# Attention followed by a rational feed-forward network on one core: VectorE runs both heads' passes over the scores in a row, ahead of the copies that read the transposes

## The chip, the core and the metric

The kernel runs on one core of a Trainium2 chip. A core has five engines with queues of their own that are worked off in order: TensorE (PE in the rows, PEld for its weight loads), VectorE (DVE), ScalarE (ACT), GpSimd (POOL) and SyncE (SP, which here only issues DMAs). They meet at semaphores alone. The metric is the device time of one execution in microseconds; less is better.

## The reference, cut to what matters

```
scores = (q @ k^T) / 8 + bias(head, i, j)      # B=4, H=8, S=576, D=64, f32
attn   = softmax(scores)                       # over j
x      = (attn @ v), heads side by side        # 2304 x 512
h      = x @ w_in                              # 2304 x 2048
g      = P(h) / Q(h)                           # cubic over quadratic
out    = g @ w_out                             # 2304 x 512
```

The bias is a small network of the distance of i and j. It is the same for all batches, so the kernel first writes it to DRAM as tables.

## The kernel before, in words

The first stage (lines 561 to 659) makes the bias tables. The second is attention, the third the feed-forward network. The change touches attention alone.

Attention works on units. A unit is a pair of heads of one batch: 16 units. A unit has 576 query rows; rows come in blocks of 128, and two units share one block for their last 64 rows. So there are 72 steps, nine for every two units (the list `steps`; NS is 72). In step i the function `step_a` writes out work of four different blocks, so that each engine has something of another block to do:

- TensorE: the scores of block i (`e_qk`, line 324): head 0 of the pair uses rows 0 to 63 of the array, head 1 rows 64 to 127. The scores come in two halves of 288 columns, in the order head 0, head 1, head 0, head 1. Each f32 product is two records in the trace, so a step has 8. Then the transposes of the probabilities of block i-2 (`e_tp`, line 393; 18 of them), then the product with v of block i-3 (`e_pv`, line 433; 20 records).
- VectorE: one pass over each head's scores (`e_ttr`, line 334): it adds the bias, writes -scores to `s2` and takes the row minimum into `m`. Between the pass of head 0 and that of head 1 stand the "tails" of block i-2 (line 412, and line 416 where a unit ends): copies of the last transposes out of the accumulator tile `mx`. Behind both stand the reciprocals of the row sums where a unit ends (`e_recip`, lines 360 and 361), the copy of block i-3's product with v out of `mx` (line 443), and at last one of three passes that split weights into a high and a low part (lines 130, 138, 144; the "weight pass", given out one to a step by `run_jobs`).
- ScalarE: the exponential of head 1 of block i-1 (line 350), a rebias of the weights in every third step (line 135), the copy of block i-2's other transposes out of the tile `tp` (line 401), and the exponential of head 0 of block i.
- GpSimd multiplies a finished unit by the reciprocals (`e_norm`) and subtracts for the low weights. SyncE issues the loads of q, k, v, bias and weights and the stores, in the order in which the program writes them.

What sets the order around the change are the buffers. The scores have one tile for each head (`ps_sc`, two buffers), so head j's scores of step i+1 can't start before head j's pass of step i is through. `mx` has one buffer: the transposes of step i+1 write it when the copies at lines 412 and 443 of step i have read it. The tails wait for TensorE's last write of `mx` that was written out ahead of them, which is the last record of the product with v at line 433, although they read other columns. The tile `s2` has three buffers, so head 1's pass of step i reuses what the exponential of head 0 of step i-1 has read.

Of the kernel before, what the change touches and what calls it, by code (L numbers as in the profile page):

```python
# [33 lines left out]
def tile_attn_moe(  # L34
# [183 lines left out]
    with tc.manual_schedule():  # L218
# [3 lines left out]
        with ExitStack() as actx:  # L222
# [54 lines left out]
            def split_x(n_, k, x=None):  # L277
                if k == 0:
                    pool = xps[n_ % 2]
                    xh[n_] = pool.tile([P, KD, TT], F32R, tag="xh", name=f"xh{n_}")  # L280
                    xl[n_] = pool.tile([P, KD, TT], F32R, tag="xl", name=f"xl{n_}")
                hi, lo = (v[n_][:, k, :] for v in (xh, xl))
                x = xr[n_][:, k, :] if x is None else x
                return (
                    lambda: A.copy(out=hi, in_=x),
                    lambda: V.tensor_tensor(out=lo, in0=x, in1=hi.bitcast(F32), op=ALU.subtract),  # L286
                )
# [23 lines left out]
            def e_qk(i):  # L311
                u, c = steps[i]
                for j in range(2):
                    sc[i, j] = ps_sc.tile([P, 2, 512], F32, tag="sc", name=f"sc{i}_{j}")
                if c < 4:
                    ops = [(u, slice(c * P, c * P + P), slice(0, P))]
                else:
                    ops = [(u + z, slice(512, S), slice(64 * z, 64 * z + 64)) for z in range(2)]
                for a in range(2):
                    for j in range(2):  # L320
                        r = slice(64 * j, 64 * j + 64)
                        for n, x, o in ops:
                            q, k = qk[n]
                            T.matmul(  # L324
                                sc[i, j][o, a, :SH], q[r, x], k[r, a * SH:(a + 1) * SH],
                                start=True, stop=True,
                            )

            def e_ttr(i, j):
                u, c = steps[i]  # L330
                p, b = units[u]
                t = epool.tile([P, S], F32, tag="s2", name=f"s2_{i}_{j}", bufs=3)
                m = epool.tile([P, 1], F32, tag="m", name=f"m{i}_{j}", bufs=4)
                V.tensor_tensor_reduce(  # L334
                    out=t.rearrange("p (a s) -> p a s", a=2),
                    in0=sc.pop((i, j))[:, :, :SH],
                    in1=bias[p][:, 5 * j + c, :].rearrange("p (a s) -> p a s", a=2),
                    scale=-0.125, scalar=3.0e38,
                    op0=ALU.add, op1=ALU.min, accum_out=m,
                )  # L340
                s2[i, j] = (t, m)

            def e_exp(i, j):
                u, c = steps[i]
                if j == 0:
                    prob[i] = epool.tile([P, 2 * S], F32, tag="p", name=f"p{i}")
                t, m = s2.pop((i, j))
                k = 4 * j + c if c < 4 else 8 + j
                z = 1 - j
                A.activation(  # L350
                    out=prob[i][:, z * S:z * S + S], in_=t, func=AF.Exp,
                    bias=m, scale=-1.0, accum_out=sums[u % 4][:, k:k + 1],
                )
# [4 lines left out]
            def e_recip(u):  # L358
                sm = sums[u % 4][:, 0:nsum(u)]
                V.tensor_scalar(out=sm, in0=sm, scalar1=1e-9, scalar2=None, op0=ALU.add)  # L360
                V.reciprocal(out=sm, in_=sm)

            def load_rb(u):
                t = rb[u] = npool.tile([P, S], F32, tag="rb", name=f"rb{u}", bufs=1)
                z = 64 * (u % 2)
                for j in range(2):
                    o = t[64 * j:64 * j + 64]
                    r, rl = rsum[u], rsum[u - u % 2]
                    nc.sync.dma_start(
                        out=o[:, 0:512].rearrange("d (c s) -> d c s", c=4),  # L370
                        in_=r[4 * j:4 * j + 4, :].unsqueeze(0).to_broadcast([64, 4, P]),
                    )
                    nc.sync.dma_start(
                        out=o[:, 512:S],
                        in_=rl[8 + j:9 + j, z:z + 64].to_broadcast([64, 64]),
                    )

            def e_norm(u):
                x = xs.pop(u)
                p, b = units[u]  # L380
                eng = V if u == NX else G
                eng.tensor_tensor(out=x, in0=x, in1=rb.pop(u), op=ALU.mult)
                nc.sync.dma_start(out=xd[b][:, p, :], in_=x)
# [71 lines left out]
            def run_act():  # L455
                while actq:
                    actq.pop(0)()
# [10 lines left out]
            def loads(i):  # L468
                g, c = divmod(i, UPG)
                if i == 1:  # L470
                    load_qk(1, nc.scalar)
                    load_v(1, nc.scalar)
                for u, x, y in ((2 * g + 2, 0 if g else 4, 3 if g else 6), (2 * g + 3, 5 if g else 7, 8)):
                    if u < NU and c == x:
                        load_qk(u)
                    if u < NU and c == y and u != 3:
                        load_v(u)
                if i == UPG + 1:
                    load_v(3)
                p, r = divmod(i, 2 * UPG)  # L480
                r = {2: 0, 7: 1, 11: 2, 13: 3, 16: 4}.get(r)
                if r is not None and p + 1 < NP:
                    load_bias(p + 1, r)
                if i == NS - 14:
                    load_x(0, 0, 0, KD - 1)
                if i == NS - 6:
                    load_x(1, 1, 0, KD - 1)

            def step_a(i):
                def ok(d):  # L490
                    return 0 <= i - d < NS

                if i < NS:
                    loads(i)
                first = []
                if NS - i in (11, 9, 7):
                    first = split_x(0, (11 - NS + i) // 2)
                elif i == NS - 5:
                    first = split_x(0, KD - 1, x12[0][:, :TT])
                if first:  # L500
                    first[0]()
                    later.append(first[1])
                while len(later) > (1 if first else 0):
                    later.pop(0)()
                if ok(0):
                    e_qk(i)
                if ok(1):
                    e_exp(i - 1, 1)
                run_act()
                if i >= TL:  # L510
                    mx = ps_mx.tile([P, 2, 512], F32, tag="mx", name=f"mx{i}")
                tails = pv = None
                if ok(TL):
                    tails = e_tp(i - TL, mx)
                if i == NS + 1:
                    mm1(0, 1)
                if ok(TL + 1):
                    pv = e_pv(i - TL - 1, mx)
                if ok(0):
                    e_ttr(i, 0)  # L520
                if tails:
                    tails()
                if ok(0):
                    e_ttr(i, 1)
                    e_exp(i, 0)
                if ok(1):
                    u, c = steps[i - 1]
                    if c == (3 if u % 2 else 4):
                        e_recip(u)
                if i == NS - 1:  # L530
                    mm1(0, 0)
                if i == NS + 1:
                    load_x(1, 1, KD - 1, KD)
                g, c = divmod(i - TL, UPG)
                if g > 0:
                    u = 2 * g - 2
                    if c == 0 and u != NX:
                        e_norm(u)
                    if c == 5 and g * 2 < NU:
                        e_norm(u + 1)  # L540
                    if c == 1 and u + 1 < NU - 1:
                        load_rb(u + 1)
                if i == NS - 7:
                    x12.append(xs[NX])
                    e_norm(NX)
                if g < NU // 2 and c == (6 if g else 8):
                    load_rb(2 * g)
                if i == NS + TL:
                    load_rb(NU - 1)
                if pv:  # L550
                    pv()
                if i >= 2:
                    run_jobs(i >= 5 and (c > 0 or g % 2 == 0))
# [383 lines left out]
```

## Time and profile before

| | us |
|---|---|
| median of 3 runs | 766.61 (766.08 to 766.80) |
| the profiled execution | 766.36 |
| its span | 764.6 |
| steps 6 to 69 of attention (63 steps) | 71.53 to 338.39 |
| attention's end and the feed-forward network | 338.39 to 764.60 |

The profiled execution took 1.8 us more than its span, for what lies around it. A step is counted here from the start of head 0's pass over the scores to that of the next step: 266.86 us for 63 steps, 4.24 us each. All times in the rows are microseconds from the start of the span.

### The profile page before, as it was taken

Reading aid. Unit: us, or ns where it says so; the run is one execution under the profiler, and the core shown is the slowest. Engines: PE = TensorE matmul, PEld = TensorE weight load, DVE = VectorE, ACT = ScalarE, POOL = GpSimd, SP = SyncE. Lnnn points to the kernel's source line nnn. Section 1 sums busy time; section 2 is a strip of 40 time slices with the busy share of each in tenths; the row PEclk is TensorE's granted clock in tenths of the full one; section 3 lists DMA queues with packets and bytes.
Section 4 is the critical chain, followed back from the end, with each engine's and each line's share of the span. In section 5 each row is a group of like instructions: output and inputs, shape, how many; then the busy total and the mean of one; then the engine's idle time right before and its main releaser. Section 6 shows DMA issues by size and latency. Waiting matters only on the chain.

```text
span 764.6 us, 16662 instructions
## 1 busy us (share of the span) xinstructions
PE 715.1 (94%) x6450; PEld 599.4 (78%) x6450; DVE 574.5 (75%) x1032; ACT 495.0 (65%) x758; POOL 232.8 (30%) x144
## 2 busy tenths in 40 slices
PE   7998888888888888888999999999999999999997
PEld 4766666666666666667989989989998998999896
DVE  7985555655565556663999999999997878787766
ACT  6887666666767666766765767576675656556552
POOL 0010121211212121111634554545544444543442
PEclk9999999999999999999999999999999999999999
DMA  5787687675858777561445433337972122130121
GB/s 178 282 310 273 197 274 234 201 224 180 276 156 274 210 233 243 170 192 47 148 140 174 168 125 125 132 143 235 311 251 85 41 83 80 46 123 35 50 83 42
DMA packets 77583, 129.50 MB, mean 169 GB/s; under 512 B 12208, under 2 KB 33856, under 8 KB 77504
## 3 DMA queue, kind: packets, MB, share of 16 engines
q1 hardware_dynamic: 76640, 126.77, 50.9%
q10 hardware_dynamic: 864, 1.67, 0.7%
q8 instruction: 51, 0.84, 0.4%
q14 instruction: 28, 0.23, 0.1%
HBM read 89.65 MB, written 35.61 MB: 164 GB/s over the span
## 4 chain that ended last, share of the span: by engine, by line
PE 55%; DVE 5%; issue 1%; ACT 0%; POOL 0%; DVEq 0%; POOLq 0%
PE o L767 24%; PE h L300 24%; PE mx L433 3%; PE sc L324 2%; PE tp L393 1%; DVE s L334 1%; DVE gh L715 1%; DVE m L722 0%; PE mx L393 0%; DVE t L705 0%; DVE xl L286 0%; DVE pt L412 0%; DVE wk L144 0%; DVE t L708 0%; POOL gl L736 0%
## 5 line engine op out<-in xcount | busy, mean ns | idle before, releaser
L324 PE MATMUL sc<-k,q 64*128 64x288 f32 (+1 forms) x640 | 138.5, 434 | 37.1 <-DVE m L334 25.6
L697 POOL TENSOR_TENSOR u<-u,w 128x768 f32<-128x768 f32 x48 | 96.6, 2013 | 162.3 <-ACT u L695 162.3
L324 PEld LDWEIGHTS sc<-k,q 64*128 64x128 f32 (+1 forms) x640 | 69.6, 174 | 83.7 <-issue 75.3
L350 ACT ACTIVATE p<-s,m 128x576 f32<-128x576 f32 x144 | 111.8, 776 | 33.0 <-DVE m L334 32.7
L334 DVE CUSTOM_DVE_ANT_0 s<-sc,bias 128x576 f32<-128x576 f32 x144 | 107.9, 750 | 23.2 <-PE sc L324 16.1
L401 ACT COPY pt<-tp 128x1024 f32<-128x1024 f32 x72 | 72.9, 1012 | 66.5 <-PE tp L393 66.4
L694 ACT ACTIVATE w<-h 128x768 f32<-128x768 f32 x48 | 39.0, 813 | 101.6 <-PE h L300 101.6
L736 POOL TENSOR_TENSOR gl<-m,r 128x768 fp32r<-128x768 f32 x47 | 87.2, 1856 | 57.5 <-DVE m L729 55.4
L412 DVE COPY pt<-mx 128x128 f32<-128x128 f32 x72 | 21.0, 291 | 106.7 <-PE mx L433 106.7
L300 PE MATMUL h<-xl,wih 128*128 128x384 f32 x288 | 97.0, 337 | 0.3 <-DVE xl L286 0.3
L300 PE MATMUL h<-xh,wih 128*128 128x384 f32 x288 | 97.3, 338 | 0.0
L300 PE MATMUL h<-xh,wil 128*128 128x384 f32 x288 | 97.0, 337 | 0.0
L433 PE MATMUL mx<-pt,v 128*64 128x128 f32 (+1 forms) x1600 | 95.1, 267 | 0.9 <-DVE xs L443 0.9
L767 PE MATMUL o<-woh,gh 128*128 128x512 f32 x216 | 85.3, 395 | 0.0
L767 PE MATMUL o<-wol,gh 128*128 128x512 f32 x216 | 85.1, 394 | 0.0
L433 PEld LDWEIGHTS mx<-pt,v 128*64 128x64 f32 x1600 | 78.6, 137 | 6.0 <-ACT u L695 1.1
L393 PE MATMUL tp<-ident,p 64*128 64x64 f32 x1152 | 74.7, 228 | 0.0
L701 ACT ACTIVATE r<-u,qc 128x768 f32<-128x768 f32 x48 | 45.1, 940 | 36.7 <-POOL u L697 36.4
L705 DVE TENSOR_TENSOR t<-t,h 128x768 f32<-128x768 f32 x48 | 45.5, 949 | 30.4 <-ACT t L696 24.9
L393 PEld LDWEIGHTS tp<-ident,p 64*128 64x128 f32 x1152 | 61.8, 139 | 6.2
L722 DVE SCALAR_TENSOR_TENSOR m<-u,qc,gh 128x768 f32<-128x768 f32 x48 | 61.7, 1285 | 5.0
L729 DVE SCALAR_TENSOR_TENSOR m<-t,cst,m 128x768 f32<-128x768 f32 x48 | 64.2, 1337 | 1.7
(73 smaller groups left out, 1354.6 us busy)
## 6 DMA issues: line engine op xcount, KB each, us to landing
tab<-e SPq DMA_DIRECT2D x36, 295.5 KB, 4.2
wx<-in_w_in_dram SPq DMA_DIRECT2D x16, 512.0 KB, 5.1
wy<-in_w_in_dram SPq DMA_DIRECT2D x16, 512.0 KB, 4.3
wx<-in_w_out_dram SPq DMA_DIRECT2D x16, 512.0 KB, 3.9
wy<-in_w_out_dram SPq DMA_DIRECT2D x16, 512.0 KB, 5.2
xr<-xd SPq DMA_DIRECT2D x7, 768.0 KB, 6.2
ws<-wh SPq DMA_DIRECT2D x20, 256.0 KB, 2.2
ws<-wl SPq DMA_DIRECT2D x20, 256.0 KB, 2.9
```

The lines of the kernel that those rows point to most:

```text
L300: T.matmul(hps[s][:, j, :TT], w[:, k, sl], x[:, k, :], start=(k == 0 and z == 0), stop=(k == KD - 1 and z == 2),)
L324: T.matmul(sc[i, j][o, a, :SH], q[r, x], k[r, a * SH:(a + 1) * SH], start=True, stop=True,)
L334: V.tensor_tensor_reduce(out=t.rearrange("p (a s) -> p a s", a=2), in0=sc.pop((i, j))[:, :, :SH], in1=bias[p][:, 5 * j + c, :].rearrange(" ...
L350: A.activation(out=prob[i][:, z * S:z * S + S], in_=t, func=AF.Exp, bias=m, scale=-1.0, accum_out=sums[u % 4][:, k:k + 1],)
L393: T.transpose(out, pb[x, k0:k0 + P], ident[x, x])
L401: A.copy(out=t[:, 0:8].rearrange("p x (r s) -> p r x s", r=2), in_=ps)
L433: T.matmul(ps[y, o], vt[n][:, kc, y], t[:, 2 * kc + j if kc < 4 else 8, o], start=(kc == 0), stop=(kc == 4),)
L697: G.tensor_tensor(out=u, in0=u, in1=w, op=ALU.mult)
L722: V.scalar_tensor_tensor(out=m, in0=rt[s, "u"], scalar=qc, in1=rt[s, "gh"].bitcast(F32), op0=ALU.add, op1=ALU.mult,)
L729: V.scalar_tensor_tensor(out=m, in0=rt[s, "t"], scalar=abs_[:, 0:1], in1=m, op0=ALU.add, op1=ALU.subtract)
L736: eng.tensor_tensor(out=lo, in0=rt[s, "m"], in1=rt[s, "r0"], op=ALU.mult)
L767: T.matmul(po[n, c], l[:, j, c * P:(c + 1) * P], r[fp][:, j, :], start=(first and x is a), stop=(last and x is z),)
```

## The change

In each step, head 1's pass over the scores (`e_ttr(i, 1)`) now stands directly behind head 0's, and the tails stand behind the reciprocals and GpSimd's norms and the loads that go with them, directly ahead of the copy of the product with v. No instruction is added or taken out.

```
                 if ok(0):
-                    e_ttr(i, 0)
-                if tails:
-                    tails()
-                if ok(0):
-                    e_ttr(i, 1)
+                    for j in range(2):
+                        e_ttr(i, j)
                     e_exp(i, 0)
                 if ok(1):
                     u, c = steps[i - 1]
...
                 if g < NU // 2 and c == (6 if g else 8):
                     load_rb(2 * g)
+                if tails:
+                    tails()
                 if i == NS + TL:
                     load_rb(NU - 1)
                 if pv:
```

VectorE's queue in step 41, before. `s2_41_0` is written by the pass of head 0 (its second row reads out the minimum), `s2_41_1` by that of head 1, `pt39` by the tails, `xs8` by the copy of the product with v, `wh5` by the weight pass:

```order
L334 ISA s2_41_0_3333,m41_0_3334<-sc41_0_3292,bias2_2016 128x576
L334 ISA m41_0_3334 128x1
L412 COPY pt39_3302<-mx41_3301 128x128
L334 ISA s2_41_1_3337,m41_1_3338<-sc41_1_3293,bias2_2016 128x576
L334 ISA m41_1_3338 128x1
L360 TENSOR_SCALAR sum0_113<-sum0_113 128x10
L361 RECIPROCAL sum0_113<-sum0_113 128x10
L443 COPY xs8_3209<-mx41_3301 128x128
L138 SCALAR_TENSOR_TENSOR wh5_1_3299<-wx5_1_3048,wh5_1_3299 128x512
```

The same step on VectorE, after:

```order
L334 ISA s2_41_0_3333,m41_0_3334<-sc41_0_3292,bias2_2016 128x576
L334 ISA m41_0_3334 128x1
L334 ISA s2_41_1_3336,m41_1_3337<-sc41_1_3293,bias2_2016 128x576
L334 ISA m41_1_3337 128x1
L360 TENSOR_SCALAR sum0_113<-sum0_113 128x10
L361 RECIPROCAL sum0_113<-sum0_113 128x10
L412 COPY pt39_3302<-mx41_3301 128x128
L443 COPY xs8_3209<-mx41_3301 128x128
L138 SCALAR_TENSOR_TENSOR wh5_1_3299<-wx5_1_3048,wh5_1_3299 128x512
```

The copy out of `mx` moved from between the two passes to behind the reciprocals; the rest kept its order.

TensorE's queue in step 42, before, with the semaphores that a row waits for. `sc42_0` and `sc42_1` are the scores of the two heads, `p40` the probabilities that are transposed, `pt39` what the product with v reads:

```order
L324 MATMUL sc42_0_3346<-k9_2740,q9_2739 128x288 [waits DVE_49]
L324 MATMUL sc42_1_3347<-k9_2740,q9_2739 128x288 [waits DVE_49,PE_49]
L324 MATMUL sc42_0_3346<-k9_2740,q9_2739 128x288
L324 MATMUL sc42_1_3347<-k9_2740,q9_2739 128x288
L393 MATMUL mx42_3353<-ident_60,p40_3282 128x64 [waits DVE_49,PE_49,Activation_49]
```

And after:

```order
L324 MATMUL sc42_0_3346<-k9_2740,q9_2739 128x288 [waits DVE_49]
L324 MATMUL sc42_1_3347<-k9_2740,q9_2739 128x288 [waits DVE_49]
L324 MATMUL sc42_0_3346<-k9_2740,q9_2739 128x288
L324 MATMUL sc42_1_3347<-k9_2740,q9_2739 128x288
L393 MATMUL mx42_3353<-ident_60,p40_3281 128x64 [waits DVE_49,PE_49,Activation_49]
```

TensorE's order is the same; head 1's first product no longer waits for TensorE's own earlier work (the last product with v, which the tails had waited for).

On SyncE the store of a finished unit's row sums, which belongs to the tails, moves behind loads in two places: near the start, and at the end of attention. The second, before:

```order
L419 DMA rs15_5248<-rt15_5247 8x128
L274 DMA xr1_4819<-xd0_72 128x192
L274 DMA xr1_4819<-xd1_73 128x192
L383 DMA xd2_74<-xs14_4862 128x576
L369 DMA rb15_5292<-rs15_5248 64x512
```

And after:

```order
L274 DMA xr1_4819<-xd0_72 128x192
L274 DMA xr1_4819<-xd1_73 128x192
L419 DMA rs15_5248<-rt15_5247 8x128
L383 DMA xd2_74<-xs14_4862 128x576
L369 DMA rb15_5292<-rs15_5248 64x512
```

The last unit's sums are stored behind two loads of the feed-forward network's input instead of ahead of them.

## Rows read from the trace of the kernel before

**Rows 1.** The page's first part: busy time, share of the span, instructions.

```profile
PE 715.1 (94%) x6450; PEld 599.4 (78%) x6450; DVE 574.5 (75%) x1032; ACT 495.0 (65%) x758; POOL 232.8 (30%) x144
```

**Rows 2.** Stretches: length, busy PE, PEld, DVE, ACT, POOL, granted clock, DMA share, GB/s.

```profile
71.53:338.39 266.86, 233.83 (x3128) 178.79 (x3127) 159.95 (x494) 180.92 (x339) 40.91 (x31) 1.00 0.71 225
338.39:349.44 11.05, 9.91 (x155) 7.97 (x152) 5.08 (x18) 6.70 (x12) 4.07 (x3) 1.00 0.24 80
349.44:764.60 415.16, 408.12 (x2114) 368.25 (x2112) 352.82 (x363) 253.56 (x320) 184.43 (x96) 1.00 0.37 122
...
93.30:110.00 16.70, 14.74 (x198) 10.96 (x196) 9.41 (x30) 11.20 (x21) 2.34 (x3) 1.00 0.88 281
68.30:76.70 8.40, 7.40 (x104) 5.26 (x102) 4.79 (x14) 5.96 (x12) 0.00 (x0) 1.00 1.01 382
```

**Rows 3.** Timeline of TensorE in one step: start, length, what, [idle before <- releaser].

```profile
217.76 0.75 PE L324 MATMUL sc<-k,q 64*128 64x288 f32 x2
218.99 0.96 PE L324 MATMUL sc<-k,q 64*128 64x288 f32 x5 [0.48 <-DVE m L334]
...
221.92 0.51 PE L324 MATMUL sc<-k,q 64*128 64x288 f32 x1
```

**Rows 4.** Timeline of VectorE in the same step.

```profile
217.88 0.29 DVE L412 COPY pt<-mx 128x128 f32<-128x128 f32 x1 [1.55 <-PE mx L433]
218.09 0.75 DVE L334 CUSTOM_DVE_ANT_0 s<-sc,bias 128x576 f32<-128x576 f32 x1
218.76 0.08 DVE L334 DVE_READ_ACCUMULATOR2_ANT m<- 128x1 f32 x1
218.76 0.28 DVE L443 COPY xs<-mx 128x128 f32<-128x128 f32 x1
218.96 0.42 DVE L130 TENSOR_SCALAR wk<-wx 128x512 uint32<-128x512 uint32 x1
219.89 0.76 DVE L334 CUSTOM_DVE_ANT_0 s<-sc,bias 128x576 f32<-128x576 f32 x1 [0.51 <-PE sc L324]
```

**Rows 5.** Whole span by line, the scores: busy, mean ns, idle before and releasers.

```profile
L324 PE MATMUL sc<-k,q 64*128 64x288 f32 (+1 forms) x640 | 138.5, 434 | 37.1 <-DVE m L334 25.6 <-DVE sum L360 7.2 <-DVE xs L443 3.3
```

**Rows 6.** Timeline of TensorE in the first steps of attention (0 and 3).

```profile
49.95 1.24 PE L324 MATMUL sc<-k,q 64*128 64x288 f32 x8
...
57.91 1.33 PE L324 MATMUL sc<-k,q 64*128 64x288 f32 x8 [1.03 <-DMA k<-in_kt_dram]
58.95 0.22 PE L393 MATMUL mx<-ident,p 64*128 64x64 f32 x1
...
60.96 0.75 PE L324 MATMUL sc<-k,q 64*128 64x288 f32 x2
```

**Rows 7.** Timeline of VectorE in step 0.

```profile
51.22 0.76 DVE L334 CUSTOM_DVE_ANT_0 s<-sc,bias 128x576 f32<-128x576 f32 x1 [0.90 <-PE sc L324]
...
51.90 0.75 DVE L334 CUSTOM_DVE_ANT_0 s<-sc,bias 128x576 f32<-128x576 f32 x1
```

**Rows 8.** By line, 71.53 to 338.39, ScalarE and VectorE: columns as in rows 5.

```profile
L350 ACT ACTIVATE p<-s,m 128x576 f32<-128x576 f32 x126 | 97.9, 777 | 28.7 <-DVE m L334 28.7
L401 ACT COPY pt<-tp 128x1024 f32<-128x1024 f32 x63 | 63.8, 1012 | 57.0 <-PE tp L393 56.9
...
L135 ACT ACTIVATE wh<-wk,wmin 128x512 uint32<-128x512 uint32 x20 | 14.2, 712 | 0.4 <-DVE wk L130 0.4
...
L138 DVE SCALAR_TENSOR_TENSOR wh<-wx,wh 128x512 uint32<-128x512 uint32 x20 | 13.6, 679 | 0.0
```

**Rows 9.** A load of weights: issue on SyncE, its use on VectorE, median to landing.

```profile
270.80 0.37 SPq L120 DMA_DIRECT2D wx<-in_w_in_dram  x1
...
286.78 0.42 DVE L130 TENSOR_SCALAR wk<-wx 128x512 uint32<-128x512 uint32 x1
...
wx<-in_w_in_dram SPq DMA_DIRECT2D x16, 512.0 KB, 5.1
```

**Rows 10.** DMA view, 71.53 to 338.39.

```profile
DMA packets 34451, 59.96 MB, mean 225 GB/s; under 512 B 7529, under 2 KB 13927, under 8 KB 34414
```

More of the change, by code (lines that the diff above doesn't have):

```diff
@@ L519, in step_a @@
                 if ok(0):
[L520 to L524, printed above, removed]
+                    for j in range(2):
+                        e_ttr(i, j)
                     e_exp(i, 0)
@@ L547, in step_a @@
                     load_rb(2 * g)
+                if tails:
+                    tails()
                 if i == NS + TL:
```

## The prediction

> **What bounds the kernel now.** I read the busy shares first [rows 1]: TensorE is busy for 94% of the span, which would leave little to gain. The stretches say where the rest lies [rows 2]. From 349.44 us on TensorE is busy for 408.12 of 415.16 us; the change has nothing there. In steps 6 to 69 of attention it is busy for 233.83 of 266.86 us, and no other engine is full either: VectorE 159.95, ScalarE 180.92, the DMA engines 71%. That points to a loop of waits. I looked for it in one step, engine by engine.
>
> TensorE first [rows 3]: head 0's first scores at 217.76, then nothing can start before 218.99, then the rest of the scores, the transposes, the product with v, and the next step at 221.92. The period is 4.16 us. VectorE says what was waited for [rows 4]: it had been idle for 1.55 us until the last product with v ended, did the tails at 217.88, then head 1's pass at 218.09, whose minimum is read out by 218.84; then head 1's scores go at 218.99. So the loop is: product with v ends, tails, head 1's pass, head 1's scores, transposes, product with v. It costs 218.99 - 217.76 = 1.23 us ahead of the scores of head 1, and 221.92 - 218.99 = 2.93 us for the rest. Head 1's pass had its data long before: the scores it reads were done ahead of the transposes. It stood behind a wait that is not its own.
>
> The trace reports only part of that as idle time: 37.1 us before the scores in the whole span, 36.1 of it for VectorE [rows 5], about half a microsecond a step. The other 0.75 us is booked as busy, since head 0's first product runs there. It runs alone, though, and the two heads need not run one after the other: in step 0, where both score tiles were free, all 8 records took 1.24 us from 49.95 [rows 6], while two records alone take 0.75 us [rows 3].
>
> **The change, part by part.** *The two passes in a row.* Head 1's pass starts when head 0's is through. Step 0 has this order already, since it has no tails [rows 7]: the scores start at 49.95 [rows 6], the passes at 51.22 and 51.90, the second of 0.75 us. From scores to both tiles free: 2.70 us. As a loop of its own (scores, two passes, next scores) that is about 2.8 us, with the 0.15 us from the read-out to the start of the matmul [rows 3, 4] (218.84 to 218.99).
>
> *TensorE's own work in a step.* With both tiles free, the scores of both heads run side by side. In the old step the part from 218.99 on [rows 3] holds four records of head 1 in a row, and so everything that the new step needs: 2.93 us. Step 3 shows a whole step with both tiles free [rows 6]: 57.91 to 60.96, 3.05 us, with the heads a little apart. I take 2.96, near the lower one, since step 3 started on a late load of k; 3.05 stays as the other end. That is longer than VectorE's loop of 2.8 us, so TensorE becomes the bound among the engines, and the price of the loop falls by 4.24 - 2.96 = 1.28 us a step.
>
> *The tails and what stands behind them.* They still wait for the product with v. It ends just after the next step's scores have started (the tails start 0.12 us after the scores [rows 3, 4]). After that VectorE does the tails, the copy and the weight pass: 0.21 + 0.20 us by their starts [rows 4] (217.88 to 218.09, 218.76 to 218.96), and 0.42 us [rows 4] or 0.68 us [rows 8] for the weight pass. The copies are through about 0.55 us after the scores' start. Their reader, the next transposes into `mx`, starts 1.04 us after it (57.91 to 58.95 in step 3 [rows 6]). So the single `mx` costs nothing. With a weight pass of 0.68 us VectorE is free 1.2 us after the scores' start, about when the next pass has its data (51.22 - 49.95 = 1.27 us). The cover is thin, but the gate for head 1's scores has 0.15 us of room.
>
> *Other edits.* The reciprocals now run ahead of the tails, while VectorE waits for the product with v; they cost nothing. The store of the row sums moves behind loads on SyncE at two places; its readers come two steps later. Both at zero.
>
> *ScalarE.* In the stretch its busy time is 180.92 us, 2.87 us a step, of which two exponentials, a copy and a third of a rebias [rows 8]. Its waits, 28.7 us for the minimum and 57.0 us for the transposes, shrink with the loop. At 2.96 us a step it is 97% busy: not the bound, but without slack in the steps with a rebias.
>
> *The DMA engines.* This is the term that decides. All loads are issued step by step, so a shorter step asks for the same work in less time. The share of 0.71 over 266.86 us is 189.5 us of work with all 16 engines full. TensorE's floor is 63 x 2.96 = 186.5 us. So DMA would have to run at full share throughout to keep up. It did reach 1.01 for 8.4 us, and 0.88 over 16.7 us [rows 2]. What evens it out is that loads come early: a load of weights is issued 16.0 us before its use and lands in 5.1 us [rows 9]. I take a share of 0.90: 189.5 / 0.90 = 210.5 us. The bounds are full share, where TensorE's floor takes over, and 0.79, not far above today's 0.71.
>
> The Trainium skill ("DMA: Bandwidth & Descriptors", Specifications) counts bytes: about 358 GB/s of HBM for a core. By that the 59.96 MB of the stretch [rows 10] need 167 us, DMA is no bound, and the time is that of the first rival below. The rows speak for counting packets instead: 382 GB/s was reached in one stretch, and 281 GB/s in another at a share of 0.88; 13,927 of 34,451 packets are under 2 KB.
>
> *The sum.* Steps 6 to 69: 266.86 - 210.5 = 56.4 us less. From 338.39 to 349.44 the DMA share is 0.24, so there the loop falls to TensorE's floor: 11.05 / 4.24 = 2.6 steps at 1.28, less some of the drain, 3.2 us. The steps before 71.53 I leave as they are, since DMA is full from 68.3. Together 59.6. The profiled execution's 766.36 becomes 706.8 (0.25 us below the median of the runs, which I neglect).
>
> **The rivals.**
> *All of it is kept (DMA evens out).* The loads' lead of 16 us against 5.1 us to landing speaks for it; that TensorE, ScalarE and DMA would all have to be over 95% full at once speaks against it. 63 steps at 2.96 to 3.05 us are 186.5 to 192 us, so 75 to 80 us less, and 3.2 more at the end: 683 to 688 us.
> *Only the idle time goes.* If head 0's early product was useful work and not lost time, the gain is the reported wait of 36.1 us: 730 us. For it: that is what the waits say. Against it: step 3's whole step in 3.05 us.
> *The weights come late, and it gets slower.* VectorE's queue is in order, and the weight pass stands ahead of the next step's pass over the scores. If a load of weights isn't there, both heads' scores stop. The lead of 16.0 us is 3.8 steps, so 11.2 us at the new pace. A job of weights takes three steps, which gain 3 x 1.28 = 3.8 us. So when loads land 15.0 us after their issue, all gain is gone; at 15.4 us, 20 jobs cost 8 us more: 774 us. It takes three times today's median, and the total of DMA work doesn't grow, so a late load can't stay late; I give it little.
> *The wait only moves* (head 1's scores still behind the tails by the same semaphore): no change. The order of TensorE's queue says no: the wait on its own products is gone.
>
> **How the numbers follow.** A measurement of this kernel can tell 0.2%, 1.5 us, from no change. Chances: DMA paces attention at shares of 0.85 to 0.97, 691 to 720 us: 0.55. All of it is kept, 681 to 691: 0.17. Only the idle time, or a DMA share near 0.79, 720 to 740: 0.17. A smaller gain up to 764: 0.05. No change: 0.02. Slower: 0.04. The bounds of the DMA term are 683 us at TensorE's floor and 736 us at a share of 0.79. The range from 683 to 736 holds the first, most of the second and most of the third, and leaves out some 0.18.
>
> **What would show it right or wrong.** In the new trace VectorE's two passes should stand 0.68 us apart in every step, the idle time should be ahead of the tails alone, TensorE's scores should come as 8 records in about 1.3 us with no wait for VectorE between them. The step should be 3.0 to 3.4 us, with a DMA share of 0.85 or more and now and then a wait for a load of weights, q or k. If the share stays under 0.85 and steps are above 3.2 us all the same, DMA isn't what paces it, and I have missed a loop, likely one through ScalarE. If steps are 3.7 us, the scores didn't run side by side.

## The result and the profile after

The changed kernel took 693.01 us (median of 4 runs, 691.35 to 695.80) against 766.42 us: a ratio of 0.9046, with a 95% interval from 0.9016 to 0.9076. The forecast was 706.8 us in a range from 683 to 736. The profiled execution took 693.02 us, with a span of 691.2. Steps 6 to 69 now lie between 71.98 and 268.17: 196.19 us in place of 266.86, 3.11 us a step.

The page's first part, as [rows 1], and the stretches, as [rows 2] (length, busy PE, PEld, DVE, ACT, POOL, clock, DMA share, GB/s):

```profile
PE 671.3 (97%) x6450; PEld 577.8 (84%) x6450; DVE 578.1 (84%) x1032; ACT 484.8 (70%) x758; POOL 233.8 (34%) x144
...
71.98:268.17 196.19, 191.89 (x3090) 158.31 (x3092) 163.32 (x495) 171.37 (x339) 41.36 (x31) 0.99 0.91 300
268.17:275.14 6.97, 6.97 (x139) 6.06 (x137) 4.79 (x16) 5.43 (x13) 2.64 (x2) 1.00 0.74 247
275.14:691.20 416.06, 409.33 (x2132) 369.29 (x2128) 353.30 (x365) 254.61 (x321) 185.96 (x97) 1.00 0.36 122
```

In steps 6 to 69 TensorE is now busy for 191.89 of 196.19 us, and the DMA share went from 0.71 to 0.91. VectorE's busy time hardly moved (159.95 to 163.32 us): no work was saved on the engine whose order was changed. The sum closes: 70.67 us in steps 6 to 69, 3.14 us from there to the end, and 0.45 us lost ahead of step 6 make 73.36 us, the difference of the two spans (764.57 and 691.21).

One step on TensorE, to be held against [rows 3]:

```profile
177.96 1.24 PE L324 MATMUL sc<-k,q 64*128 64x288 f32 x8
179.03 0.22 PE L393 MATMUL mx<-ident,p 64*128 64x64 f32 x2
179.09 0.67 PE L393 MATMUL tp<-ident,p 64*128 64x64 f32 x16
179.69 1.31 PE L433 MATMUL mx<-pt,v 128*64 128x128 f32 x20
180.93 0.51 PE L324 MATMUL sc<-k,q 64*128 64x288 f32 x2
```

And on VectorE, as [rows 4]:

```profile
178.08 0.29 DVE L412 COPY pt<-mx 128x128 f32<-128x128 f32 x1 [0.42 <-PE mx L433]
178.29 0.28 DVE L443 COPY xs<-mx 128x128 f32<-128x128 f32 x1
178.48 0.42 DVE L130 TENSOR_SCALAR wk<-wx 128x512 uint32<-128x512 uint32 x1
179.34 0.76 DVE L334 CUSTOM_DVE_ANT_0 s<-sc,bias 128x576 f32<-128x576 f32 x1 [0.44 <-PE sc L324]
180.03 0.08 DVE L334 DVE_READ_ACCUMULATOR2_ANT m<- 128x1 f32 x1
180.03 0.75 DVE L334 CUSTOM_DVE_ANT_0 s<-sc,bias 128x576 f32<-128x576 f32 x1
```

The scores are one block of 8 records with nothing waited for in between. The step takes 180.93 - 177.96 = 2.97 us. VectorE's passes stand 0.69 us apart; it waits for the product with v only ahead of the tails, and for 0.42 us in place of 1.55, and once more, for 0.44 us, for the scores themselves.

By line over the whole span, the scores, as [rows 5]:

```profile
L324 PE MATMUL sc<-k,q 64*128 64x288 f32 (+1 forms) x640 | 92.6, 428 | 4.0 <-DVE m L334 4.0
```

The wait ahead of the scores fell from 37.1 to 4.0 us, and their busy time from 138.5 to 92.6 us, though a record takes as long as before (428 against 434 ns). That is the sign of products side by side: the same records cover less time. (Busy times of one line count time that it shares with other lines; for TensorE as a whole, in steps 6 to 69, the idle time fell from 33.0 to 4.3 us and the busy time from 233.8 to 191.9, together the 70.67 us.)

What is new is ScalarE's wait. By line, 71.98 to 268.17, as [rows 8]:

```profile
L350 ACT ACTIVATE p<-s,m 128x576 f32<-128x576 f32 x126 | 96.9, 773 | 0.1
L401 ACT COPY pt<-tp 128x1024 f32<-128x1024 f32 x63 | 63.2, 1004 | 14.1 <-PE tp L393 13.9
...
L135 ACT ACTIVATE wh<-wk,wmin 128x512 uint32<-128x512 uint32 x20 | 14.4, 718 | 12.3 <-DVE wk L130 3.9 <-DMA wih<-wh 3.7 <-DMA ws<-wh 3.5
```

The waits for minimum and transposes went from 85.7 to 14.2 us. The rebias of the weights, which had waited 0.4 us, now waits 12.3 us, most of it for stores that still read the buffer it writes.

### The profile page after: what moved, and what is told of

The parts are those of the page before. It is cut to its first block, busy times and chain, and to the rows that moved or that the text cites. A ratio compares the mean times of both kernels' runs of the same rounds, so it can differ in the third digit from the quotient of the medians.

```text
span 691.2 us, 16655 instructions
## 1 busy us (share of the span) xinstructions
PE 671.3 (97%) x6450; PEld 577.8 (84%) x6450; DVE 578.1 (84%) x1032; ACT 484.8 (70%) x758; POOL 233.8 (34%) x144
## 3 DMA queue, kind: packets, MB, share of 16 engines
q10 hardware_dynamic: 864, 1.67, 0.8%
## 4 chain that ended last, share of the span: by engine, by line
PE 85%; DVE 5%; DMA 4%; issue 2%; ACT 2%; SPq 1%; POOL 0%; DVEq 0%; ACTq 0%; POOLq 0%
PE o L766 27%; PE h L300 27%; PE mx L433 11%; PE sc L324 10%; PE tp L393 5%; PE pb L635 5%; DMA wih<-wh 2%; DVE ring L597 1%; DVE gh L714 1%; DMA ws<-wh 1%; PE mx L393 1%; DMA wy<-in_w_in_dram 1%; ACT pt L401 1%; DMA cst<-in_cst_dram 1%; DMA tab<-e 1%
## 5 line engine op out<-in xcount | busy, mean ns | idle before, releaser
L334 DVE CUSTOM_DVE_ANT_0 s<-sc,bias 128x576 f32<-128x576 f32 x144 | 103.6, 754 | 18.7 <-PE sc L324 11.5
L324 PE MATMUL sc<-k,q 64*128 64x288 f32 (+1 forms) x640 | 92.6, 428 | 4.0 <-DVE m L334 4.0
L324 PEld LDWEIGHTS sc<-k,q 64*128 64x128 f32 (+1 forms) x640 | 50.3, 175 | 24.4 <-DVE m L334 9.1
L714 DVE SCALAR_TENSOR_TENSOR gh<-t,cst,r 128x768 fp32r<-128x768 f32 x48 | 56.5, 1176 | 8.2 <-ACT r L701 5.8
L766 PE MATMUL o<-woh,gl 128*128 128x512 f32 x216 | 56.2, 395 | 0.0
L300 PEld LDWEIGHTS h<-xl,wih 128*128 128x128 f32 x288 | 54.1, 188 | 2.1 <-DVE xl L286 0.7
```

The source lines that it names most:

```text
L300: T.matmul(hps[s][:, j, :TT], w[:, k, sl], x[:, k, :], start=(k == 0 and z == 0), stop=(k == KD - 1 and z == 2),)
L324: T.matmul(sc[i, j][o, a, :SH], q[r, x], k[r, a * SH:(a + 1) * SH], start=True, stop=True,)
L334: V.tensor_tensor_reduce(out=t.rearrange("p (a s) -> p a s", a=2), in0=sc.pop((i, j))[:, :, :SH], in1=bias[p][:, 5 * j + c, :].rearrange(" ...
L714: V.scalar_tensor_tensor(out=hi, in0=rt[s, "t"], scalar=abs_[:, 0:1], in1=rt[s, "r0"], op0=ALU.add, op1=ALU.mult,)
L766: T.matmul(po[n, c], l[:, j, c * P:(c + 1) * P], r[fp][:, j, :], start=(first and x is a), stop=(last and x is z),)
```

## The experiments

Three questions: is it really the two heads running side by side that made the gain larger than the reported wait; is the swap with the tails all of the change; and do DMAs pace attention now, as the forecast had it?

**Are the heads' products worth more side by side? (e1, e2)** Both kernels with the scores' loops exchanged:

```
-                for a in range(2):
-                    for j in range(2):
+                for j in range(2):
+                    for a in range(2):
```

> The changed kernel, with the scores written out head by head (both halves of head 0, then both of head 1), so that the two heads' products can't run side by side. My reading (most of the gain is head 0's and head 1's products running side by side, and not the idle time): a step's scores take some 0.95 us longer, the step 3.9 us in place of 3.11, the time 740 to 750 us. Rival (only the idle time was gained): the order of the products doesn't matter, 690 to 700 us.

> The kernel before with the same edit of the scores' order. My reading: its loop runs through head 1's pass and then four records of head 1 in a row, and head 0's products fall into the wait, so the step stays 4.2 us and the time 762 to 770 us. Rival (the order of the products costs the same in both kernels): about 50 us more than before, 815 us.

The changed kernel took 691.5 us, the other 766.7 us (one execution each, as in e4 and e9 to e12). The first is what the rival expected, and not because the rival is right: the edit didn't do what I meant. TensorE in a step of e1:

```profile
160.22 1.25 PE L324 MATMUL sc<-k,q 64*128 64x288 f32 x8
161.30 0.23 PE L393 MATMUL mx<-ident,p 64*128 64x64 f32 x2
```

Four records of head 0 stand first in the queue, and still all 8 take 1.25 us: head 1's first record starts 14 ns behind head 0's first. That these two are of different heads follows from e9 below, whose only further edit puts both heads on the same rows: there the records follow one another, the first head's four ahead of the other's. So TensorE lets products in the other half of its rows pass. The order in the program therefore can't tell the two readings apart; a semaphore that isn't there yet can hold a product back, and so can the same half of the rows. In e2 the semaphore does, and all four records of head 0 run in the wait:

```profile
205.31 1.24 PE L324 MATMUL sc<-k,q 64*128 64x288 f32 x4
206.72 0.48 PE L324 MATMUL sc<-k,q 64*128 64x288 f32 x1 [0.18 <-DVE m L334]
```

The reported wait shrinks to 0.18 us here (over the whole span to 4.8 us, from 37.1), and the step is as long as before (4.23 us). A wait in the trace thus says little about what its end is worth: in e2 it is filled with head 0's work, and the loop through head 1's pass is the same.

**The same question, put better (e9, e10).** Both heads' scores from one half of the rows, on top of the exchanged loops:

```
-                        r = slice(64 * j, 64 * j + 64)
+                        r = slice(0, 64)
```

> The changed kernel with the scores of both heads taken from the array's rows 0 to 63 (head 1's scores are then head 0's, so head 1's result is left out) and written out head by head: now the products can't run side by side. In e1 they did so whatever their order, since TensorE started products of the other row group past those ahead of them. My theory (the gain is more than the idle time because both heads' products run side by side): a step's scores take some 0.97 us more, the step about 3.95 us, the time 740 to 750 us. Rival (only the idle time counts): 690 to 700 us.

> The kernel before with the same edit. My theory: head 0's products fall into the wait for head 1's pass, so it costs nothing there, the step stays at 4.2 us, 762 to 772 us. Rival (the same cost in both kernels): 810 to 820 us.

748.6 us and 767.3 us, 3.96 and 4.25 us a step: both as expected. TensorE in a step of the changed kernel:

```profile
200.74 1.72 PE L324 MATMUL sc<-k,q 64*128 64x288 f32 x6
202.06 0.27 PE L393 MATMUL mx<-ident,p 64*128 64x64 f32 x1
...
203.42 1.31 PE L433 MATMUL mx<-pt,v 128*64 128x128 f32 x20
204.67 0.70 PE L324 MATMUL sc<-k,q 64*64 64x288 f32 x4
```

And in the kernel before:

```profile
201.75 1.95 PE L324 MATMUL sc<-k,q 64*128 64x288 f32 x6
...
205.97 0.51 PE L324 MATMUL sc<-k,q 64*128 64x288 f32 x1
```

In the first the 8 records follow one another, the transposes' second half is pushed back, and the step is 204.67 - 200.74 = 3.93 us. In the second they do so too, and the step is 205.97 - 201.75 = 4.22 us. So running side by side is worth 748.6 - 693.0 = 55.6 us in the changed kernel and about nothing (767.3 us, and 766.9 for the kernel before measured beside it) in the old one, where head 0's products had a wait to fall into. Without it, the swap would have gained 18 us of the 73, less than the 36 us of reported wait.

**Is the swap all of it? (e3, e6, with the changed kernel again as e5)** Only this much of the change:

```
                     e_ttr(i, 0)
+                    e_ttr(i, 1)
                 if tails:
                     tails()
                 if ok(0):
-                    e_ttr(i, 1)
```

> The kernel before with the tails moved behind head 1's pass and nowhere further: they stay ahead of the exponential, the reciprocals, the norms and the row sums' loads. My reading (the swap of tails and pass is all of the change): as the changed kernel, 689 to 697 us. Rival (the rest of the move counts): over 700 us.

It took 701.2 us (696.21 to 703.50), a ratio of 0.9132 (0.9080 to 0.9183), against 0.9046 for the changed kernel measured at another time. That is over 700, as the rival expected. Its trace has the same step (a median of 3.03 us against 3.02), but one place where several steps are lost. ScalarE there:

```profile
122.32 0.76 ACT L350 ACTIVATE p<-s,m 128x576 f32<-128x576 f32 x1
122.98 0.19 ACT L350 ACTIVATION_READ_ACCUMULATOR p<-s,m 128x1 f32 x1
127.69 0.72 ACT L135 ACTIVATE wh<-wk,wmin 128x512 uint32<-128x512 uint32 x1 [4.52 <-DMA woh<-wh]
```

A store of weights landed late, the rebias waited, and the copies and exponentials behind it with it. To see whether that belongs to the order, both ran side by side on one chip:

> The changed kernel once more, beside the next three on the same chip, since moving the tails alone came out 8 us above it in another call. If the places of the rest count: 691 to 696 us and the next one 8 us more. If it was the chip: both within 4 us of each other.

> The kernel before with only the tails moved behind head 1's pass, as before. Theory 1 (the swap is all; late stores differ from chip to chip): within 4 us of the changed kernel in this call. Theory 2 (reciprocals ahead of the tails matter, or the row sums' store): 6 to 10 us above it.

694.6 us (ratio 0.9056, 0.9039 to 0.9072) and 695.6 us (0.9062, 0.9042 to 0.9082): no difference that the runs can tell. So the swap gives 71 of the 72 us here, and 65 in e3; it is nearly all of the change. The chip alone, though, doesn't explain e3. The trace of e6, taken from the longest of its four executions (698.17 us), shows the same wait for the same store, and the trace of the changed kernel beside it a shorter one; ScalarE in e6, then in e5:

```profile
128.69 0.72 ACT L135 ACTIVATE wh<-wk,wmin 128x512 uint32<-128x512 uint32 x1 [5.48 <-DMA woh<-wh]
```

```profile
122.56 0.72 ACT L135 ACTIVATE wh<-wk,wmin 128x512 uint32<-128x512 uint32 x1 [2.79 <-DMA woh<-wh]
```

In the first trace of the changed kernel it is 0.41 us. Whether the places of the reciprocals, norms and stores are worth a few microseconds by way of this store stays open.

**Do DMAs pace attention? Less DMA work (e4).** The weight loads of the later jobs are left out:

```
         def load():
+            if 0 < f < KF - LATE:
+                st.update(first[part])
+                return
...
+            if f == 0:
+                first[part] = dict(st)
```

> The changed kernel with the weight loads of attention left out but for the first two jobs; the later jobs split the first job's weights again, so 18 MB of 60 MB of DMA and the result of these weights are left out, and all work of the engines stays. DMA theory (lateness of DMAs makes the step 3.11 us where TensorE's own work is 2.97): no more waits for stores of weights, steps 2.95 to 3.0 us, 684 to 688 us. Rival (ScalarE's own work makes the difference): no change, 690 to 696 us.

688.6 us, between the two ranges, with a median step of 3.01 us. ScalarE's rebias waits for no store any more. Its stretch of steps 6 to 69:

```profile
71.85:264.15 192.30, 190.94 (x3090) 159.15 (x3091) 165.13 (x494) 172.15 (x338) 41.26 (x31) 0.99 0.67 209
```

With the DMA share down to 0.67 TensorE is busy for 99% of the stretch, and it is 192.30 us long. Late DMAs thus cost some 4 of the 196.19 us of the changed kernel; the rest is TensorE's own. The 688.6 us alone wouldn't show it, since it is one execution and the changed kernel's own lie between 691.35 and 695.80. What shows it is the stretch: in the traces of the changed kernel (its own and e5's) and of e1 it is 195.3 to 196.3 us long. TensorE's idle time in it is 1.36 us here, 4.30 in the changed kernel and 5.70 in e5.

**More DMA work (e11, e12).** A copy of 512 KB for each of the 20 jobs, in both kernels:

```
+            if f < KF - LATE:
+                d = dpool.tile([P, 2 * FN], U32, tag=f"ex{f}_{part}", name=f"ex{f}_{part}")
+                nc.sync.dma_start(out=d, in_=w.bitcast(U32)[f])
```

> The changed kernel with a copy of 512 KB from DRAM to DRAM added to each of the 20 weight jobs of attention; nothing reads it. At 4 KB packets of 0.2 us each on 16 engines one copy is 1.6 us of all engines, 18 of them in steps 6 to 69 about 29 us. DMA theory (attention runs with the DMA engines nearly full): steps 3.5 us or more, 715 to 732 us. Rival (TensorE alone paces): under 700 us.

> The kernel before with the same copies added. DMA theory: its DMA share of 0.71 has room for them (0.82 with them), so the time stays, 765 to 772 us. Rival (added DMA work costs the same wherever it is): 15 us or more above the kernel before.

711.6 us, 3 us short of the range (steps of 3.39 us where 3.5 or more were expected), and 766.5 us, as expected. A stretch of the changed kernel that holds steps 6 to 69 but for the last microsecond (they lie from 73.46 to 287.05 in its trace), and that of the other:

```profile
72.50:286.00 213.50, 198.03 (x3078) 161.80 (x3079) 163.31 (x491) 169.66 (x336) 41.52 (x31) 0.96 0.96 322
```

```profile
71.53:338.39 266.86, 233.62 (x3120) 178.23 (x3120) 160.32 (x494) 180.39 (x338) 40.91 (x31) 1.00 0.81 263
```

The copies cost 18.6 us in one kernel and nothing in the other, where they only raise the share to 0.81. Not all of the 18.6 us is waiting: TensorE is idle for 15.5 us of this stretch (4.3 in the changed kernel), and its busy time is 6.1 us longer, at a granted clock of 0.96 in place of 0.99. So the changed kernel stands close to where DMA takes over as the bound, and the old one stood far from it. With 0.96 over 213.50 us, a share near one can be held for long, which [rows 2] hadn't shown.

**Can the late DMAs' cost be had? (e7, e8)** A third buffer for the rebiased weights, and the first loads of weights issued ahead of attention:

```
-            A.activation(out=tl("wh", U32, 2), in_=st["wk"], func=AF.Relu, bias=wmin, scale=8.0)
+            A.activation(out=tl("wh", U32, 3), in_=st["wk"], func=AF.Relu, bias=wmin, scale=8.0)
...
-                t = pt[i] = epool.tile([P, 9, P], F32, tag="pt", name=f"pt{i}")
+                t = pt[i] = epool.tile([P, 9, P], F32, tag="pt", name=f"pt{i}", bufs=2)
```

> The changed kernel with three buffers in place of two for the rebiased weights (wh), so that ScalarE's rebias doesn't wait for the store of two jobs earlier; for room, the transposed probabilities (pt) have two buffers in place of three, which cost no wait in the order of the queues. DMA-lateness theory: ScalarE's 8.2 us of waits for stores go, steps 3.05, 3 to 7 us less than the changed kernel. Rival (DMA throughput as such paces, and the wait only shows it): another wait takes its place, within 2 us.

```
-        seq = [("sp", j[0]) for j in jobs[:2]]
+        seq = []
...
+                jobs01 = bg[:2]
                 bg = in_order(bg, after)
...
+                    if y in (14, 16):
+                        jobs01[(y - 14) // 2][0]()
```

> The changed kernel with the first two jobs' weight loads issued in the table stage (at its 15th and 17th row) in place of step 2. If the stall at step 6 (4.3 us on the first weights, and a slow TensorE clock for some 4 us behind it) is what I take it for: VectorE's wait for wx goes, no slow clock, 4 to 7 us less than the changed kernel. Rival (another late DMA, such as q and k behind the bias, stands there next): within 2 us.

694.1 us (ratio 0.9046, 0.9004 to 0.9089) and 694.1 us (0.9055, 0.9038 to 0.9072), beside 694.6 us for the changed kernel measured with them: both as the rivals expected, though e7's own executions lie between 689.19 and 697.54 us, so that a gain of 3 us there can't be told from none. The rebias waits for no store in e7, and ScalarE's longest wait for a DMA is another one. In e8 the first weights are there, and TensorE waits for a late k three steps earlier. ScalarE's waits in e7 (in total, times, longest), then TensorE in e8 and in the changed kernel beside it (e5):

```profile
ACT xh L285 <- DMA xr<-xd: 8.6, 3, 6.4
```

```profile
62.05 1.72 PE L324 MATMUL sc<-k,q 64*128 64x288 f32 x8 [2.38 <-DMA k<-in_kt_dram]
```

```profile
58.31 2.15 PE L324 MATMUL sc<-k,q 64*128 64x288 f32 x8 [1.56 <-DMA k<-in_kt_dram]
```

The wait for k isn't new in e8: e5 has it too, shorter by 0.8 us. What else e8 pays is a later start: its first pass over the scores is at 53.70 us and that of e5 at 51.09, since the loads now stand among the stores of the bias tables (ScalarE's waits for those went from 0.8 to 2.6 us). Its steps 6 to 69 take 194.67 us against 196.34 in e5, so what is gained there is spent ahead of it.

No version that does all the work beats the changed kernel by more than the measurement tells.

## Why the prediction was right or wrong

*The loop.* Right. Product with v, tails, head 1's pass, head 1's scores was the bound, and its end is gone from the rows.

*Head 0's early product as lost time.* Right, and the term of the sum that mattered most: of the 70.67 us in steps 6 to 69, 28.7 us were TensorE's idle time and 41.9 us its busy time. The rival "only the idle time goes" (730 us) fell with the 693 us; e9 and e10 say why. (Its 36.1 us are those of the whole span; steps 6 to 69 hold 33.0 of them, so it stood for 733 us.)

*TensorE's floor of 2.96 us.* The plain step is 2.97 us. The median is 3.02, since steps in which a unit ends or two units share a block do more (3.12 to 3.14 us in e4, three steps in nine); e4's 192.30 us for 63 steps is 3.05 with all that and the slow clock behind step 6. My other end of 3.05 was nearer for a whole stretch. (VectorE's loop, put at about 2.8 us, adds up to 2.70 + 0.15 = 2.85; it is still below the floor.)

*The tails and the weight pass behind the product with v, the single `mx`, the reciprocals:* at zero, as costed. The next pass over the scores waits for the scores, not for VectorE.

*ScalarE.* At nothing, as costed: it is busy for 171.37 of 196.19 us, 87% and not the 97% that I feared.

*The DMA term.* This is the step that was mis-sized: 210.5 us forecast, 196.19 measured. The share was near my 0.90 (0.91), but the work was less: 0.91 x 196.19 = 178.5 us where I had put 0.71 x 266.86 = 189.5. Some work left the stretch (58.83 MB against 59.96), and the rest is time in which a packet of the old kernel occupied its engine for longer: 225 GB/s at a share of 0.71 is 317 GB/s at full share, 300 at 0.91 is 330. Most of it is in the packets of 4096 B, 202 ns in the mean before and 187 after (195 in e5). I took the share for work that can't shrink. Why these packets took longer isn't shown; a light load alone doesn't explain it, since in e12, at a share of 0.81, they still took 199 ns. With 178.5 us of work TensorE is the bound (e4), and DMA only makes it stumble, for 4 us. So DMA doesn't pace attention, which was the case that the number rested on. The forecast's number was 13.8 us too high, the time lies at the edge of the case that I called likeliest (691 to 720), and the mechanism is closer to the first rival, in which all is kept (683 to 688): that one lacked the 4 us of late DMAs. That the time fell into the likeliest case, by 2 us, is in part luck: in that case DMA sets the step, and here TensorE does, with some microseconds of late DMAs on top.

*The byte count of the Trainium skill* ("DMA: Bandwidth & Descriptors", Specifications) pointed to the first rival, since 358 GB/s leaves room for the 60 MB. The stretch agrees: it ran at 300 GB/s, with TensorE as the bound. e11 can't tell bytes from packets as the measure. Its engines were full (0.96) at 322 GB/s, but its copies read DRAM and write it; with both sides counted (18 copies of 0.524 MB in 213.5 us are 44 GB/s more) it is some 366 GB/s, an estimate.

*The steps ahead of 71.53.* I left them at zero for full DMA engines, and they lost 0.45 us. What happened is, on a small scale, the rival in which the weights come late. VectorE in the changed kernel:

```profile
67.03 0.28 DVE L443 COPY xs<-mx 128x128 f32<-128x128 f32 x1
71.63 0.43 DVE L130 TENSOR_SCALAR wk<-wx 128x512 uint32<-128x512 uint32 x1 [4.32 <-DMA wx<-in_w_in_dram]
```

The first weights, issued at 66.85 behind the bias, came 4.32 us late, and the pass over the scores stood behind them. TensorE then waited 2.94 us, and soon after it went on its granted clock fell from 1.00 (2.4 GHz) to 0.50 (1.2 GHz):

```profile
72.79 2.09 PE L324 MATMUL sc<-k,q 64*128 64x288 f32 x7 [2.94 <-DVE m L334]
```

```profile
74.00:76.00 2.00, 2.00 (x21) 1.52 (x20) 1.67 (x4) 1.24 (x4) 0.00 (x0) 0.50 1.03 407
```

Seven records took 2.09 us where eight take 1.24. Most of that isn't the clock: head 1's scores started 0.68 us behind head 0's, since its pass had just run, and in e5 seven records behind a late pass took 1.67 us (from 72.61) at a granted clock of 1.00. What steps 3 to 5 had gained was lost here. Later loads of weights came in time, as their lead of 16 us [rows 9] had promised.

*The end of attention.* 3.2 us forecast, 3.14 measured from step 69 on.

*The signs.* I had named a step above 3.2 us at a share under 0.85 as the sign of a missed loop. It didn't come, but there was a loop that I had missed: the rebias waits for stores of weights two jobs back, where it had waited 0.4 us for VectorE and for no DMA [rows 8]. What it costs by itself isn't shown: in e7 it is gone, another wait for a DMA stands in its place, and the time is the same.

## What to carry to other kernels

When an engine waits in its queue for something that isn't its next critical work, look at what stands behind the waiting instruction; moving the ready work ahead of the wait cost nothing here. Don't price the end of a wait by the idle time in the trace: work that falls into the wait, such as one head's products alone on half of the array, is booked as busy and is part of the loss, and e9 and e10 price it. And don't take a DMA share times its stretch as work that stays: it fell here from 189.5 to 178.5 us for nearly the same bytes. Find out with fewer and with more transfers where DMA takes over.

## What the runs showed of the hardware that I had not expected

Products on different halves of the array's rows don't keep the program's order: in e1 head 1's first product started 14 ns behind head 0's, past three records that stood ahead of it. So a queue "worked off in order" is too strong for TensorE. With both heads on the same half (e9) the order is kept. A wait for a semaphore keeps it too: in the kernel before, head 0's second half didn't pass head 1's first, which waited.

A stall of one engine can cost twice: behind 2.94 us without a product TensorE's granted clock was 0.50 between 74 and 76 us, while waits of half a microsecond a step in the kernel before left it at 1.00. The length of the one wait doesn't decide: behind 1.56 us in e5 the clock was 0.50 as well, and behind 2.19 us in e1, on another chip, it stayed at 1.00:

```profile
58.50:61.50 3.00, 3.00 (x28) 2.47 (x28) 0.97 (x3) 0.86 (x4) 0.00 (x0) 0.50 0.24 40
```

```profile
72.20 1.43 PE L324 MATMUL sc<-k,q 64*128 64x288 f32 x6 [2.19 <-DVE m L334]
70.00:80.00 10.00, 7.81 (x106) 6.59 (x106) 7.98 (x25) 7.95 (x15) 1.29 (x1) 1.00 1.04 394
```
